# Decode attention with an MLP on one Trainium2 core: Wq loaded in column chunks, heads in h-major order, and the output projection's matmuls inside the loop

## The chip, the cores and the metric

The kernel runs on one core of one Trainium2 chip. The metric is the time of one execution on the device in microseconds (us), as the median of several runs; lower is better. "Span" is the length of the one execution that the profiler recorded.

## The reference

Four rows (a batch of 4, one new token each) go through a pre-norm attention block with a cache of 4096 keys and 32 heads of 128, then through an MLP with the Mish activation. All arrays are bf16. K and V are 134 MB each; they are nearly all of the 283.4 MB that the kernel has to read.

```python
def _A_ref(x, k_cache, v_cache, wq, wo):
    B, Sq, D = x.shape                      # 4, 1, 640
    H, Dh = 32, 128
    q = (x @ wq).reshape(B, Sq, H, Dh).transpose(0, 2, 1, 3)
    scores = jnp.einsum("bhqd,bhkd->bhqk", q, k_cache) * (Dh ** -0.5)
    p = _softmax(scores, axis=-1)
    o = jnp.einsum("bhqk,bhkd->bhqd", p, v_cache)
    return o.transpose(0, 2, 1, 3).reshape(B, Sq, H * Dh) @ wo

h  = x + _A_ref(_layernorm(x), k_cache, v_cache, wq, wo)
h2 = h + _B_ref(_layernorm(h), w1, b1, w2)  # 640 -> 1728, mish, -> 640
```

## The kernel before

There are 128 (row, head) pairs; I call each a head. For one head, K is a tile of 128 partitions with 32 keys each. VectorE multiplies it with the broadcast query and adds the 128 products of each key in a tree of halvings. ScalarE takes the exponential. TensorE multiplies with V and puts the four partial rows together. In cuts:

```python
wq_sb = big.tile([128, DC, H * Dh], BF16, tag="w40k")          # 40 KB a partition
nc.sync.dma_start(out=wq_sb, in_=A_wq...)                      # one DMA, ahead of K
...
for rnd in range(2):                                           # all of Q first
    for n in range(4):
        for c in range(DC): nc.tensor.matmul(qall_ps[...], xT[:, c, :], wq_sb[...])
    nc.vector.tensor_copy(out=Qall[...], in_=qall_ps)
wo_sb = big.tile([128, DC, H * Dh], BF16, tag="w40k")          # Wo takes Wq's place
...
heads = [(b, h) for b in range(N) for h in range(H)]
for idx, (b, h) in enumerate(heads):
    issue_qbc(idx + PRE)                                       # broadcast q to 128 partitions
    Kt = kt_pool.tile(...)   # 3 buffers, 1 MB, on the SyncE queue
    Vt = v_pool.tile(...)    # 3 buffers, 1 MB, on the ScalarE queue
    prod = work.tile([128, RC, Dh], BF16, tag="prod")          # 2 buffers
    nc.vector.tensor_tensor(out=prod, in0=Kt, in1=qbc..., op=ALU.mult)
    # tree: 128 -> 64 -> 32 -> 16 -> 8 -> 4 -> 2, then s_f32
    # ... exp, row sums, 8 PV matmuls, pvsb, 4 o matmuls, Orow
    if h == H - 1:           # once per row: reciprocal, 32 transposes -> OT_sb[:, :, b]
# behind the loop
for h in range(H):
    for (c0, c1) in ((0, 512), (512, D)):
        nc.tensor.matmul(yatt_ps[:, c0:c1], lhsT=OT_sb[:, h, :], rhs=wo_view[:, h, c0:c1], ...)
# ... h_rows, layernorm, MLP on 4 partitions x 1728, out
```

The program is written in this order, but the order in which each engine runs its instructions is made by a scheduler when the program is compiled.

The softmax here doesn't subtract the row's maximum and nothing guards it: scores larger than these inputs give would overflow.

Of the kernel before, what the change touches and what calls it, by code (L numbers as in the profile page):

```python
# [8 lines left out]
FP32 = mybir.dt.float32  # L9
BF16 = mybir.dt.bfloat16  # L10
# [5 lines left out]
def kernel(  # L16
# [13 lines left out]
    nc = tc.nc  # L30

    B, Sq, D = A_x.shape
    _, H, Sk, Dh = A_k_cache.shape
    F = B_w1.shape[1]
    N = B * Sq
    DC = D // 128
    RC = Sk // 128
    GP = 4
    NG = RC // GP
    SCALE = float(Dh) ** -0.5  # L40
    EPS = 1e-5

    consts = ctx.enter_context(tc.tile_pool(name="consts", bufs=1))
    big = ctx.enter_context(tc.tile_pool(name="big", bufs=1))
    work = ctx.enter_context(tc.tile_pool(name="work", bufs=2))
# [4 lines left out]
    x_bf = consts.tile([N, D], BF16)  # L50
    nc.sync.dma_start(out=x_bf[:, :], in_=x_rows[:, :])

    wq_sb = big.tile([128, DC, H * Dh], BF16, tag="w40k")
    nc.sync.dma_start(
        out=wq_sb[:, :, :], in_=A_wq.rearrange("(c p) n -> p c n", p=128)
    )

    ident = consts.tile([128, 128], BF16)
    make_identity(nc, ident[:, :])
    ident4 = ident[0:N, 0:N]  # L60

    ones_col = consts.tile([128, 1], FP32)
    nc.vector.memset(ones_col[:, :], 1.0)
# [5 lines left out]
    for b in range(N):  # L69
        nc.vector.tensor_copy(  # L70
            out=sel4[:, b, :], in_=ident[0:N, b : b + 1].to_broadcast([N, 128])
# [29 lines left out]
    def transpose_rows(rows_bf, colT_sb, nelems, ps_pool):  # L101
        nchunk = (nelems + 127) // 128
        tp_ps = ps_pool.tile([128, nchunk * N], FP32, tag="tp_ps")
        for c in range(nchunk):
            m = min(128, nelems - c * 128)
            nc.tensor.matmul(  # L106
                tp_ps[0:m, c * N : (c + 1) * N],
                lhsT=rows_bf[0:N, c * 128 : c * 128 + m],
                rhs=ident4,
                start=True,  # L110
                stop=True,
            )
        full_chunks = nelems // 128
        if full_chunks > 0:
            nc.vector.tensor_copy(
                out=colT_sb[:, 0:full_chunks, :],
                in_=tp_ps[:, 0 : full_chunks * N].rearrange("p (c n) -> p c n", n=N),
            )
        rem = nelems - full_chunks * 128
        if rem > 0:  # L120
            nc.vector.tensor_copy(
                out=colT_sb[0:rem, full_chunks, :],
                in_=tp_ps[0:rem, full_chunks * N : (full_chunks + 1) * N],
            )

    ln1_bf = consts.tile([N, D], BF16)
# [2 lines left out]
    xT = consts.tile([128, DC, N], BF16)  # L129
    Qall = consts.tile([N, H * Dh], BF16)  # L130

    with tc.tile_pool(name="ps_pro", bufs=1, space=bass.MemoryType.PSUM) as ps_pro:
        transpose_rows(ln1_bf, xT, D, ps_pro)
        QCOLS = 2048
        for rnd in range((H * Dh) // QCOLS):
            qall_ps = ps_pro.tile([N, QCOLS], FP32, tag="qall_ps")
            for n in range(QCOLS // 512):
                col0 = rnd * QCOLS + n * 512
                for c in range(DC):
                    nc.tensor.matmul(  # L140
                        qall_ps[:, n * 512 : (n + 1) * 512],
                        lhsT=xT[:, c, :],
                        rhs=wq_sb[:, c, col0 : col0 + 512],
                        start=(c == 0),
                        stop=(c == DC - 1),
                    )
            nc.vector.tensor_copy(  # L147
                out=Qall[:, rnd * QCOLS : (rnd + 1) * QCOLS], in_=qall_ps[:, :]
            )

    OT_sb = big.tile([128, H, N], BF16)

    wo_sb = big.tile([128, DC, H * Dh], BF16, tag="w40k")
    wo_view = wo_sb.rearrange("p c n -> p (c n)").rearrange("p (h n) -> p h n", h=H)
    w1_sb = big.tile([128, DC, F], BF16)
    w2_main_c = F // 128
# [1 line left out]
    w2_tail = big.tile([128, D], BF16)  # L158
    b1_bc = big.tile([N, F], BF16)

    did_late = {"done": False}

    def load_late_weights():
        if did_late["done"]:
            return
        did_late["done"] = True
        nc.sync.dma_start(
            out=wo_view[:, :, :], in_=A_wo.rearrange("(h p) n -> p h n", p=128)
        )
        nc.sync.dma_start(  # L170
            out=w1_sb[:, :, :], in_=B_w1.rearrange("(c p) n -> p c n", p=128)
        )
        nc.gpsimd.dma_start(
            out=w2_sb[:, :, :],
            in_=B_w2[0 : w2_main_c * 128, :].rearrange("(c p) n -> p c n", p=128),
        )
        rem_rows = F - w2_main_c * 128
        nc.gpsimd.dma_start(
            out=w2_tail[0:rem_rows, :], in_=B_w2[w2_main_c * 128 : F, :]
        )  # L180
        nc.gpsimd.dma_start(out=b1_bc[:, :], in_=B_b1.partition_broadcast(N))
# [5 lines left out]
    ps_cm = tc.tile_pool(name="ps_main", bufs=1, space=bass.MemoryType.PSUM)  # L187
    ps_main = ps_cm.__enter__()

    heads = [(b, h) for b in range(N) for h in range(H)]  # L190
    qbc_tiles = {}

    def issue_qbc(idx):
        if idx >= len(heads) or idx in qbc_tiles:
            return
        b, h = heads[idx]
        qbc_ps = ps_main.tile([128, 128], FP32, tag="qbc_ps")
        nc.tensor.matmul(  # L198
            qbc_ps[:, :],
            lhsT=sel4[:, b, :],  # L200
            rhs=Qall[:, h * Dh : (h + 1) * Dh],
            start=True,
            stop=True,
        )
        qbc_bf = work.tile([128, Dh], BF16, tag="qbc_bf", bufs=4)
        nc.scalar.copy(out=qbc_bf[:, :], in_=qbc_ps[:, :])  # L206
        qbc_tiles[idx] = qbc_bf

    PRE = 3
    for i in range(PRE):  # L210
        issue_qbc(i)

    lrow_ps = None
    Orow = None
    for idx, (b, h) in enumerate(heads):
        if h == 0:
            lrow_ps = ps_main.tile([1, H], FP32, tag="lrow_ps", bufs=2)
            Orow = work.tile([1, H, Dh], BF16, tag="Orow", bufs=2)

        issue_qbc(idx + PRE)  # L220

        Kt = kt_pool.tile([128, RC, Dh], BF16, tag="Kt")
        nc.sync.dma_start(
# [6 lines left out]
            in_=A_v_cache[b, h].rearrange("(p r) d -> p r d", p=128),  # L230
        )

        qbc = qbc_tiles[idx]
        prod = work.tile([128, RC, Dh], BF16, tag="prod")
        nc.vector.tensor_tensor(  # L235
            out=prod[:, :, :],
            in0=Kt[:, :, :],
            in1=qbc[:, :].unsqueeze(1).to_broadcast([128, RC, Dh]),
# [3 lines left out]
        width = Dh  # L242
        while width > 2:
            half = width // 2
            dst_dt = BF16
            nxt = work.tile([128, RC, half], dst_dt, tag=f"tree{half}")
            nc.vector.tensor_tensor(  # L247
                out=nxt[:, :, :],
                in0=cur[:, :, 0:half],
                in1=cur[:, :, half:width],  # L250
                op=ALU.add,
            )
            cur = nxt
            width = half
# [16 lines left out]
        )  # L271

        nc.tensor.matmul(  # L273
            lrow_ps[0:1, h : h + 1],
            lhsT=rowsum[:, :],
            rhs=ones_col[:, :],
            start=True,
# [2 lines left out]

        pv_ps = ps_main.tile([GP, GP * Dh], FP32, tag="pv_ps", bufs=2)
        for g in range(NG):
            nc.tensor.matmul(  # L283
                pv_ps[:, :],
                lhsT=e_bf[:, g * GP : (g + 1) * GP],
                rhs=Vt[:, g * GP : (g + 1) * GP, :],
                start=(g == 0),
                stop=(g == NG - 1),
            )
        pvsb = work.tile([GP, GP * Dh], BF16, tag="pvsb")  # L290
        nc.scalar.copy(out=pvsb[:, :], in_=pv_ps[:, :])  # L291

        o_ps = ps_main.tile([1, Dh], FP32, tag="o_ps", bufs=2)
        for i in range(GP):
            nc.tensor.matmul(  # L295
                o_ps[:, :],
# [2 lines left out]
                start=(i == 0),  # L299
                stop=(i == GP - 1),  # L300
            )
        nc.scalar.copy(out=Orow[0:1, h, :], in_=o_ps[0:1, :])  # L302

        if idx == 64:
            load_late_weights()

        if h == H - 1:
            rl = work.tile([1, H], FP32, tag="rl")
            nc.vector.reciprocal(out=rl[0:1, :], in_=lrow_ps[0:1, :])
            rl_bf = work.tile([1, H], BF16, tag="rl_bf")  # L310
            nc.vector.tensor_copy(out=rl_bf[0:1, :], in_=rl[0:1, :])
            ot_ps = ps_main.tile([128, H], FP32, tag="ot_ps")
            for hh in range(H):
                nc.tensor.matmul(
                    ot_ps[:, hh : hh + 1],
                    lhsT=Orow[0:1, hh, :],
                    rhs=rl_bf[0:1, hh : hh + 1],
                    start=True,
                    stop=True,
                )  # L320
            nc.vector.tensor_copy(out=OT_sb[:, :, b], in_=ot_ps[:, :])

    load_late_weights()
    ps_cm.__exit__(None, None, None)
    v_cm.__exit__(None, None, None)
    kt_cm.__exit__(None, None, None)
# [1 line left out]
    mlp = ctx.enter_context(tc.tile_pool(name="mlp", bufs=1))  # L328
    ps_epi = ctx.enter_context(tc.tile_pool(name="ps_epi", bufs=1, space=bass.MemoryType.PSUM))

    yatt_ps = ps_epi.tile([N, D], FP32, tag="acc1")
    for h in range(H):
        for (c0, c1) in ((0, 512), (512, D)):
            nc.tensor.matmul(  # L334
                yatt_ps[:, c0:c1],
                lhsT=OT_sb[:, h, :],
                rhs=wo_view[:, h, c0:c1],
                start=(h == 0),
                stop=(h == H - 1),
            )  # L340
    h_rows = mlp.tile([N, D], FP32)
    nc.vector.tensor_tensor(
        out=h_rows[:, :], in0=x_bf[:, :], in1=yatt_ps[:, :], op=ALU.add
# [45 lines left out]
    actT = mlp.tile([128, FC, N], BF16)  # L389
    transpose_rows(act_bf, actT, F, ps_epi)  # L390

    y2_ps = ps_epi.tile([N, D], FP32, tag="acc1")
    for (c0, c1) in ((0, 512), (512, D)):
        for c in range(FC):
            rows = min(128, F - c * 128)
# [46 lines left out]
```

## Time and profile before

| | before |
|---|---|
| median time | 746.65 us (4 runs) |
| span of the profiled run | 746.0 us |
| bytes moved | 283.8 MB |
| VectorE busy | 653.0 us (88%) |
| TensorE busy | 485.5 us (65%) |
| first product on VectorE | 45.9 us |
| last V has landed | 688.6 us |
| `h_rows` (attention done) starts | 706.35 us |

The page cuts the span into 40 equal slices of 18.65 us. The first two lines are busy tenths of VectorE (DVE) and of the DMA engines, the third is what the DMA moved in each slice.

```profile
DVE  1079999999989999999999999999989999998155
DMA  9989999999999999999999999999999999997000
GB/s 359 401 331 423 421 422 421 422 421 421 420 421 407 423 421 421 422 420 421 420 422 421 421 416 417 420 421 416 418 394 397 423 421 422 421 422 307 1 0 0
```

From the fourth slice to the 36th, the DMA is full and moves close to 421 GB/s (three slices have 394 to 407), and VectorE is nearly full too. So both are suspects for the bound of the loop, and the first and last slices are outside it.

The next view gives stretches of the span: start and end, length, then busy time of TensorE, its weight loads, VectorE, ScalarE and GpSimd with instruction counts, the granted clock, the DMA's busy share, and GB/s.

```profile
28.00:40.00 12.00, 7.85 (x27) 2.67 (x27) 2.28 (x1) 0.00 (x0) 0.00 (x0) 1.00 1.01 420
40.00:46.00 6.00, 3.28 (x16) 1.28 (x15) 2.38 (x2) 0.27 (x1) 0.00 (x0) 1.00 0.55 186
46.00:58.00 12.00, 1.41 (x7) 0.49 (x6) 12.00 (x17) 1.70 (x7) 0.00 (x0) 0.55 1.06 395
100.00:130.00 30.00, 21.08 (x94) 7.17 (x92) 30.00 (x49) 7.41 (x30) 0.00 (x0) 0.78 1.01 421
200.00:400.00 200.00, 142.91 (x660) 48.75 (x658) 193.92 (x326) 49.22 (x200) 0.00 (x0) 0.74 1.01 420
400.00:500.00 100.00, 70.94 (x303) 23.84 (x302) 96.04 (x161) 24.99 (x101) 0.00 (x0) 0.71 1.01 420
676.00:690.00 14.00, 10.23 (x46) 3.44 (x46) 10.70 (x22) 3.46 (x15) 0.00 (x0) 0.76 0.73 271
```

At 28 to 40 us VectorE uses no K at all and the DMA still moves 420. In the loop (200 to 400) it moves 420 as well. At 40 to 46 us it falls to 186. If 422 GB/s is what the DMA can do (the full slices show 420 to 423), the time that a stretch loses is its length times (1 - rate/422): 3.4 us here, 0.8 us in the next stretch, and 5.0 us at the very end.

Two lines of the timeline show the start (start, length, engine, line, operation, output <- inputs, and in brackets the idle time before it with what ended that):

```profile
29.78 6.36 PE L140 MATMUL qall_ps<-wq_sb,xT 128*4 128x512 bf16 x20 [25.15 <-DMA wq_sb<-in_A_wq_dram]
45.90 4.49 DVE L235 TENSOR_TENSOR prod<-Kt,qbc_bf 128x4096 bf16<-128x4096 bf16 x2 [0.60 <-ACT qbc_bf L206]
```

The first Q matmul waits for all of Wq, and the first product comes only at 45.9 us. And the end:

```profile
692.48 1.24 PE L283 MATMUL pv_ps<-Vt,e_bf 128*4 128x512 bf16 x5
695.73 10.53 PE L334 MATMUL yatt_ps<-wo_sb,OT_sb 128*4 128x512 bf16 x64 [0.32 <-DVE OT_sb L321]
706.35 0.81 DVE L342 TENSOR_TENSOR h_rows<-x_bf,yatt_ps 4x640 f32<-4x640 bf16 x1 [10.68 <-PE yatt_ps L334]
722.00 10.94 DVE L376 RECIPROCAL tb<-ta 4x1728 f32<-4x1728 f32 x1
```

The last PV matmuls end at 693.7, the 64 Wo matmuls stand in the open for 10.5 us, and the MLP follows. Nothing overlaps this tail.

A head's eight VectorE operations last 5.5 us added up (2.29 for the product, 1.22 to 0.19 for each of the others), and the schedule alternates the operations of two heads. The start times in the trace show neighbours of different heads overlapping by about 85 ns; where an operation follows its own producer (as a few do at the start and the end) there is a gap of 35 ns instead.

### The profile page before, as it was taken

Reading aid. Unit: us, or ns where it says so; the run is one execution under the profiler, and the core shown is the slowest. Engines: PE = TensorE matmul, PEld = TensorE weight load, DVE = VectorE, ACT = ScalarE, POOL = GpSimd, SP = SyncE. Lnnn points to the kernel's source line nnn. Section 1 sums busy time; section 2 is a strip of 40 time slices with the busy share of each in tenths; the row PEclk is TensorE's granted clock in tenths of the full one; section 3 lists DMA queues with packets and bytes.
Section 4 is the critical chain, followed back from the end, with each engine's and each line's share of the span. In section 5 each row is a group of like instructions: output and inputs, shape, how many; then the busy total and the mean of one; then the engine's idle time right before and its main releaser. Section 6 shows DMA issues by size and latency. Waiting matters only on the chain.

```text
span 746.0 us, 6937 instructions
## 1 busy us (share of the span) xinstructions
PE 485.5 (65%) x2224; PEld 167.9 (23%) x2224; DVE 653.0 (88%) x1066; ACT 166.4 (22%) x647; POOL 3.1 (0%) x9
## 2 busy tenths in 40 slices
PE   0335767667677676766676876767676676777823
PEld 0111222222222222222222222222222222222311
DVE  1079999999989999999999999999989999998155
ACT  0002222222222222222222222222222222222110
POOL 1000000000000000000000000000000000000000
PEclk9976687776667867777876568686888866677976
DMA  9989999999999999999999999999999999997000
GB/s 359 401 331 423 421 422 421 422 421 421 420 421 407 423 421 421 422 420 421 420 422 421 421 416 417 420 421 416 418 394 397 423 421 422 421 422 307 1 0 0
DMA packets 42836, 283.82 MB, mean 380 GB/s; under 512 B 4212, under 2 KB 8316, under 8 KB 9392
## 3 DMA queue, kind: packets, MB, share of 16 engines
q1 hardware_dynamic: 23872, 146.93, 47.9%
q10 hardware_dynamic: 18432, 134.23, 43.5%
q0 software_dynamic: 496, 2.23, 0.8%
q8 instruction: 17, 0.28, 0.1%
q14 instruction: 19, 0.16, 0.1%
HBM read 283.36 MB, written 0.01 MB: 380 GB/s over the span
## 4 chain that ended last, share of the span: by engine, by line
DMA 53%; PE 28%; DVE 10%; issue 5%; ACT 2%; ACTq 0%; SPq 0%; DVEq 0%
DMA Vt<-in_A_v_cache_dram 48%; PE pv_ps L283 20%; DVE nxt L247 5%; DMA wq_sb<-in_A_wq_dram 4%; PE o_ps L295 3%; DMA Kt<-in_A_k_cache_dram 2%; ACT pvsb L291 2%; DVE tb L376 1%; PE qall_ps L140 1%; PE yatt_ps L334 1%; PE y_ps L400 1%; DVE prod L235 1%; PE h_ps L355 1%; DVE Qall L147 1%; DVE s_f L256 0%
## 5 line engine op out<-in xcount | busy, mean ns | idle before, releaser
L283 PE MATMUL pv_ps<-Vt,e_bf 128*4 128x512 bf16 x1024 | 362.3, 508 | 104.7 <-DMA Vt<-in_A_v_cache_dram 104.6
L235 DVE TENSOR_TENSOR prod<-Kt,qbc_bf 128x4096 bf16<-128x4096 bf16 x128 | 293.3, 2292 | 12.4 <-DMA Kt<-in_A_k_cache_dram 11.1
L247 DVE TENSOR_TENSOR nxt<-nxt 128x1024 bf16<-128x1024 bf16 (+4 forms) x640 | 199.2, 364 | 0.2
L247 DVE TENSOR_TENSOR nxt<-prod 128x2048 bf16<-128x2048 bf16 x128 | 156.6, 1224 | 0.0
L283 PEld LDWEIGHTS <-e_bf 128*4 128x4 bf16 x1024 | 95.5, 99 | 266.3 <-issue 222.7
L291 ACT CAST pvsb<-pv_ps 4x512 bf16<-4x512 f32 x128 | 73.4, 573 | 242.5 <-PE pv_ps L283 241.4
L295 PE MATMUL o_ps<-pvsb,ident 4*1 4x128 bf16 x512 | 58.1, 243 | 44.9 <-ACT pvsb L291 44.9
L302 ACT CAST Orow<-o_ps 1x128 bf16<-1x128 f32 x128 | 32.5, 254 | 135.9 <-PE o_ps L295 134.3
L295 PEld LDWEIGHTS <-ident 4*1 4x1 bf16 x512 | 34.9, 85 | 90.9 <-issue 86.0
L265 ACT ACTIVATE e_bf<-s_f 128x32 bf16<-128x32 f32 x128 | 28.9, 226 | 93.6 <-DVE s_f L256 93.5
L273 PE MATMUL lrow_ps<-ones_col,rowsum 128*1 128x1 f32 x256 | 25.1, 167 | 33.0 <-ACT e_bf L265 33.0
L206 ACT CAST qbc_bf<-qbc_ps 128x128 bf16<-128x128 f32 x128 | 31.4, 245 | 59.2 <-PE qbc_ps L198 42.9
L198 PE MATMUL qbc_ps<-Qall,sel 4*128 4x128 bf16 x128 | 31.5, 246 | 17.4 <-ACT qbc_bf L206 15.0
L147 DVE CAST Qall<-qall_ps 4x2048 bf16<-4x2048 f32 x2 | 4.6, 2279 | 35.8 <-PE qall_ps L140 35.8
L273 PEld LDWEIGHTS lrow_ps<-ones_col,rowsum 128*1 128x1 f32 x256 | 15.2, 88 | 76.4 <-ACT e_bf L265 57.9
L140 PE MATMUL qall_ps<-wq_sb,xT 128*4 128x512 bf16 x40 | 10.8, 435 | 27.5 <-DMA wq_sb<-in_A_wq_dram 25.2
L198 PEld LDWEIGHTS <-sel 4*128 4x128 bf16 x128 | 11.9, 94 | 59.5 <-issue 55.4
L256 DVE TENSOR_TENSOR s_f<-nxt 128x32 f32<-128x32 bf16 x128 | 24.2, 189 | 0.2
L265 ACT ACTIVATION_READ_ACCUMULATOR e_bf<-s_f 128x1 f32 x128 | 23.8, 186 | 0.0
L106 PE MATMUL tp_ps<-ident,act_bf 4*128 4x4 bf16 (+1 forms) x14 | 0.6, 166 | 20.8 <-DVE act_bf L386 20.8
L140 PEld LDWEIGHTS <-xT 128*4 128x4 bf16 x40 | 3.8, 94 | 34.2 <-issue 30.1
L376 DVE RECIPROCAL tb<-ta 4x1728 f32<-4x1728 f32 x1 | 10.9, 10940 | 0.0
(49 smaller groups left out, 69.0 us busy)
## 6 DMA issues: line engine op xcount, KB each, us to landing
Vt<-in_A_v_cache_dram ACTq DMA_DIRECT2D x128, 1024.0 KB, 11.4
Kt<-in_A_k_cache_dram SPq DMA_DIRECT2D x128, 1024.0 KB, 12.4
wq_sb<-in_A_wq_dram SPq DMA_DIRECT2D x1, 5120.0 KB, 28.6
wo_sb<-in_A_wo_dram SPq DMA_DIRECT2D x1, 5120.0 KB
w_sb<-in_B_w_dram SPq DMA_DIRECT2D x1, 2160.0 KB, 36.6
w_sb<-in_B_w_dram POOLq DMA_DIRECT2D x1, 2080.0 KB, 24.5
w_tail<-in_B_w_dram POOLq DMA_DIRECT2D x1, 80.0 KB, 24.1
x_bf<-in_A_x_dram SPq DMA_DIRECT2D x1, 5.0 KB
```

Of the source, the lines that this page charges most:

```text
L140: nc.tensor.matmul(qall_ps[:, n * 512 : (n + 1) * 512], lhsT=xT[:, c, :], rhs=wq_sb[:, c, col0 : col0 + 512], start=(c == 0), stop=(c == D ...
L198: nc.tensor.matmul(qbc_ps[:, :], lhsT=sel4[:, b, :], rhs=Qall[:, h * Dh : (h + 1) * Dh], start=True, stop=True,)
L206: nc.scalar.copy(out=qbc_bf[:, :], in_=qbc_ps[:, :])
L235: nc.vector.tensor_tensor(out=prod[:, :, :], in0=Kt[:, :, :], in1=qbc[:, :].unsqueeze(1).to_broadcast([128, RC, Dh]), op=ALU.mult,)
L247: nc.vector.tensor_tensor(out=nxt[:, :, :], in0=cur[:, :, 0:half], in1=cur[:, :, half:width], op=ALU.add,)
L256: nc.vector.tensor_tensor(out=s_f32[:, :], in0=cur[:, :, 0], in1=cur[:, :, 1], op=ALU.add,)
L265: nc.scalar.activation(out=e_bf[:, :], in_=s_f32[:, :], func=ACT.Exp, scale=SCALE, accum_out=rowsum[:, :],)
L273: nc.tensor.matmul(lrow_ps[0:1, h : h + 1], lhsT=rowsum[:, :], rhs=ones_col[:, :], start=True, stop=True,)
L283: nc.tensor.matmul(pv_ps[:, :], lhsT=e_bf[:, g * GP : (g + 1) * GP], rhs=Vt[:, g * GP : (g + 1) * GP, :], start=(g == 0), stop=(g == NG - 1),)
L291: nc.scalar.copy(out=pvsb[:, :], in_=pv_ps[:, :])
L295: nc.tensor.matmul(o_ps[:, :], lhsT=ident[0:GP, i : i + 1], rhs=pvsb[:, i * Dh : (i + 1) * Dh], start=(i == 0), stop=(i == GP - 1),)
L302: nc.scalar.copy(out=Orow[0:1, h, :], in_=o_ps[0:1, :])
```

## The change

The intent: start the heads after one eighth of Wq, keep the DMA from running dry at the start, and take the Wo matmuls out of the tail. For that, heads go h-major, so that the four rows of one h are finished together. The core of the diff:

```diff
-    nc.sync.dma_start(out=wq_sb[:, :, :], in_=A_wq.rearrange("(c p) n -> p c n", p=128))
+    for n in range(NQC):                        # 8 chunks of 512 columns
+        nc.gpsimd.dma_start(out=wq_sb[:, :, n * 512 : (n + 1) * 512],
+            in_=A_wq[:, n * 512 : (n + 1) * 512].rearrange("(c p) n -> p c n", p=128))
...
-    wo_sb = big.tile([128, DC, H * Dh], BF16, tag="w40k")
+    wo_sb = big.tile([128, DC, H * Dh], BF16, tag="wo40k")     # a place of its own
+    # Wo, w1, w2, b1: all on the GpSimd queue
...
-    heads = [(b, h) for b in range(N) for h in range(H)]
+    heads = [(b, h) for h in range(H) for b in range(N)]
+    def ensure_qall(n): ...                     # Q for 512 columns, when a head needs it
...
-        prod = work.tile([128, RC, Dh], BF16, tag="prod")
+        prod = work.tile([128, RC, Dh], BF16, tag="prod", bufs=1)
-            nxt = work.tile([128, RC, half], dst_dt, tag=f"tree{half}")
+            nxt = work.tile([128, RC, half], BF16, tag=f"tree{half}", bufs=1)
...
+        if idx >= N - 1 + LAG and (idx - LAG) % N == N - 1:
+            finish_group((idx - LAG) // N, idx)    # reciprocal, 4 transposes -> OT_sb[:, h, :]
+        if idx >= 24 and yatt_next <= (idx - LAG - 2) // N - 1:
+            emit_yatt(yatt_next, idx)              # two Wo matmuls, tied behind a PV matmul
+            yatt_next += 1
...
-    for h in range(H):                             # 64 Wo matmuls behind the loop
-        for (c0, c1) in ((0, 512), (512, D)):
-            nc.tensor.matmul(yatt_ps[:, c0:c1], ...)
```

## The prediction

> **What bounds the kernel now.** The DMA. The page's 40 slices show 420 to 423 GB/s from 56 us to 670 us with DMA at 9 tenths, and 422 GB/s is also what the queues move in 28 to 40 us, when VectorE uses no K at all, so it is the DMA's own limit here [...]. 283.9 MB at 422 GB/s are 673 us. VectorE is close behind: one head's eight operations last 5.5 us added up, but the schedule alternates two heads, so that neighbours are independent and overlap by some 85 ns; a head then costs 4.85 us against 4.97 us of DMA for its 2.1 MB. Where an operation follows its own producer (a few places), a gap of 35 ns stands in place of the overlap.
>
> Outside the stream: start-up, where VectorE's first product waits until 45.9 us for all of Wq (landed at 29.8) and for the Q matmuls and casts; K and V buffers are full by then, and the DMA idles about 3.3 us (40 to 46 us by windows). At the end the last V lands at 688.6 us, PV for two backlogged heads runs to 693.8, the 64 Wo matmuls take 10.5 us (695.7 to 706.3), and the MLP another 39.7 us.
>
> **What the change does.** Same bytes. Wq comes in eight column chunks on the GpSimd queue, Q is made chunk by chunk, heads run h-major, Wo and MLP weights follow on the GpSimd queue, and Wo matmuls go into the loop.
>
> - Start: the GpSimd queue's first packets came at 6.6 us and it got 100 to 110 GB/s beside the two others. One chunk (0.66 MB) should land near 13 us (estimate), then 5 matmuls (2.1 us), copy 0.6, broadcast 0.5: first product near 17 us, not 45.9. Only the 3.3 us of DMA idleness count, since the DMA was otherwise busy.
> - Wo: 60 of 64 matmuls leave the tail: -9 us. PE has room (65% busy).
> - Slightly worse: 14.9 MB of short rows; with such rows in the mix the DMA moved 395 to 411 GB/s: +1 to 2 us.
> - VectorE: 32 short reciprocals, about 5 us in all, inside its slack. Earlier start gives it room: 1 to 2 us less hiccup (540 to 580 us ran at 397 GB/s) and less PE backlog at the end.
>
> [...]
>
> **Sum.** 746.65 - 9 - 3.3 - 3 + 1.5 = about 733 us, on the edge of 2%. Range 722 to 752. Faster by over 2%: 0.47; within 2%: 0.41; slower by over 2%: 0.12.
>
> **What would show it.** First product at 14 to 20 us; no idle DMA slice before the end; K/V progress slower than 5 us a head until the GpSimd queue is empty (about 100 us), then about 4.98; DMA ending near 684 us; h_rows some 8 us after the last V, not 17.7; the MLP tail unchanged near 40 us.
>
> **What would make it wrong.** The buffers of the product and the addition tree fall to one. If the order still alternates heads, nothing is lost: each tile is read before the next head writes it. If it becomes serial per head, a head costs about 5.7 us, VectorE bounds the loop, and the kernel reaches 780 to 800 us; in part serial, 5.1 to 5.3 us, it ends as before. Also a GpSimd queue that is served slower than I think, or reciprocals that make VectorE wait for PE.

## The result

The changed kernel takes 735.86 us (median of 10 runs, 733.82 to 736.8) against 747.15 us for the kernel before in the same rounds. The ratio is 0.9849 with a 95% interval of 0.9833 to 0.9866: faster by 1.5%, so within 2%. All ratios here are the mean time of one kernel's fast runs over that of the other's fast runs of the same rounds, so they are not quite the ratio of the medians quoted. The numerical result is correct.

The slices of the changed kernel (18.3 us each):

```profile
DVE  1996766999999999999999999999999999999564
DMA  8999999999999999999999999999999999999300
GB/s 342 418 423 422 423 414 392 421 421 421 421 421 420 422 419 422 420 422 419 416 421 422 421 413 421 419 393 422 419 419 418 414 421 417 410 415 403 121 0 0
```

Its stretches, at the same times as before:

```profile
28.00:40.00 12.00, 6.63 (x26) 1.87 (x26) 12.00 (x21) 3.76 (x10) 0.54 (x1) 1.00 1.02 418
40.00:46.00 6.00, 2.51 (x16) 0.94 (x16) 6.00 (x11) 1.50 (x8) 0.00 (x0) 1.00 1.02 427
46.00:58.00 12.00, 7.99 (x31) 2.66 (x31) 11.59 (x22) 1.73 (x10) 0.00 (x0) 0.72 1.02 425
100.00:130.00 30.00, 17.56 (x73) 5.73 (x70) 20.74 (x34) 6.00 (x27) 0.00 (x0) 0.65 1.02 399
200.00:400.00 200.00, 145.83 (x666) 52.23 (x666) 194.02 (x328) 49.70 (x211) 0.00 (x0) 0.76 1.01 420
400.00:500.00 100.00, 73.84 (x329) 26.10 (x329) 96.51 (x163) 24.56 (x105) 0.00 (x0) 0.74 1.00 414
676.00:690.00 14.00, 11.90 (x66) 4.65 (x65) 8.88 (x22) 4.34 (x17) 0.00 (x0) 0.77 0.54 191
```

The hole at 40 to 46 us is gone: 427 GB/s instead of 186. The loop moves the same 420. But 100 to 130 us now has 399 (before: 421), and 400 to 500 has 414 (before: 420); by the formula these cost 1.6 and 1.4 us more than before. (The kernel before has a weak stretch of its own at another place, the slices with 394 and 397 at 541 to 578 us.) The start and the end in the timeline:

```profile
15.90 2.29 PE L200 MATMUL qall_ps<-wq_sb,xT 128*4 128x512 bf16 x5 [10.11 <-DMA wq_sb<-in_A_wq_dram]
19.45 2.29 DVE L300 TENSOR_TENSOR prod<-Kt,qbc_bf 128x4096 bf16<-128x4096 bf16 x1 [13.09 <-ACT qbc_bf L223]
```

```profile
689.24 1.24 PE L347 MATMUL pv_ps<-Vt,e_bf 128*4 128x512 bf16 x5
692.35 0.43 PE L261 MATMUL yatt_ps<-wo_sb,OT_sb 128*4 128x512 bf16 x2 [0.25 <-ACT OT_sb L257]
692.82 0.81 DVE L388 TENSOR_TENSOR h_rows<-x_bf,yatt_ps 4x640 f32<-4x640 bf16 x1 [4.35 <-PE yatt_ps L261]
```

Three times put the gain in its place:

| | before | changed | difference |
|---|---|---|---|
| last V landed (last packet of its queue) | 688.6 | 687.6 | -1.0 |
| from there to the start of `h_rows` | 17.7 | 5.2 | -12.5 |
| from the start of `h_rows` to the end | 39.7 | 40.1 | +0.4 |
| span | 746.0 | 732.9 | -13.1 |

So the first product came 26 us earlier, but the stream of K and V ended only 1 us earlier. Added up from the two traces, what the DMA has moved by a given time puts the changed kernel ahead by 4.2 us (at 422 GB/s) at 100 us, 2.6 at 130, 2.8 at 476, 1.6 at 495, 3.8 at 580 and still 2.7 at 676. Another 1.7 us go at the very end, where the DMA is no longer full (busy 0.54 at 676 to 690 us; before 0.73): the last V is issued only when the PV matmuls of an earlier head have freed its buffer, at 683.14 us (those matmuls end at 683.04); before at 684.17 (684.00).

Nearly all of the gain is in the open tail: the Wo block (10.5 us before; two matmuls, 0.43 us together, stand there now), and TensorE is closer behind V (last PV 5.1 us after the last V before, 2.9 us now).

VectorE waits for K in both kernels, and more so now, mostly while the weights share the DMA (at 100 to 130 us it is busy 20.74 of 30 us, before 30.00). The columns are waiter, what it waited for, us in total, times, longest; first the kernel before, then the changed one:

```profile
DVE prod L235 <- DMA Kt<-in_A_k_cache_dram: 11.1, 36, 0.7
```

```profile
DVE prod L300 <- DMA Kt<-in_A_k_cache_dram: 33.5, 40, 2.8
```

### The profile page after: what moved, and what is told of

The parts are those of the page before. It is cut to its first block, busy times and chain, and to the rows that moved or that the text cites. A ratio compares the mean times of both kernels' runs of the same rounds, so it can differ in the third digit from the quotient of the medians.

```text
span 732.9 us, 7047 instructions
## 1 busy us (share of the span) xinstructions
PE 487.5 (67%) x2224; PEld 173.2 (24%) x2224; DVE 653.1 (89%) x1084; ACT 169.8 (23%) x687; POOL 12.7 (2%) x19
## 4 chain that ended last, share of the span: by engine, by line
DMA 66%; PE 23%; DVE 6%; ACT 3%; issue 2%; ACTq 0%; POOL 0%; POOLq 0%
DMA Vt<-in_A_v_cache_dram 64%; PE pv_ps L347 19%; DMA wq_sb<-in_A_wq_dram 2%; ACT pvsb L355 2%; PE o_ps L359 2%; DVE tb L422 1%; DVE nxt L311 1%; DVE prod L300 1%; PE y_ps L446 1%; PE h_ps L401 1%; PE qall_ps L200 0%; DVE act_bf L432 0%; DVE tb L413 0%; DVE h L409 0%; ACT e_bf L329 0%
## 5 line engine op out<-in xcount | busy, mean ns | idle before, releaser
L347 PE MATMUL pv_ps<-Vt,e_bf 128*4 128x512 bf16 x1024 | 356.3, 506 | 127.6 <-DMA Vt<-in_A_v_cache_dram 127.6
L311 DVE TENSOR_TENSOR nxt<-nxt 128x1024 bf16<-128x1024 bf16 (+4 forms) x640 | 201.5, 361 | 0.3 <-issue 0.2
L347 PEld LDWEIGHTS <-e_bf 128*4 128x4 bf16 x1024 | 98.5, 100 | 295.4 <-issue 248.4
L359 PE MATMUL o_ps<-pvsb,ident 4*1 4x128 bf16 x512 | 57.0, 240 | 40.6 <-ACT pvsb L355 40.5
L337 PE MATMUL grp_ps<-ones_col,rowsum 128*1 128x1 f32 x256 | 24.3, 164 | 16.3 <-ACT e_bf L329 15.9
L223 ACT CAST qbc_bf<-qbc_ps 128x128 bf16<-128x128 f32 x128 | 31.5, 246 | 13.0 <-DVE prod L300 10.9
L337 PEld LDWEIGHTS grp_ps<-ones_col,rowsum 128*1 128x1 f32 x256 | 12.4, 82 | 44.9 <-ACT e_bf L329 28.9
L200 PE MATMUL qall_ps<-wq_sb,xT 128*4 128x512 bf16 x40 | 12.7, 458 | 10.1 <-DMA wq_sb<-in_A_wq_dram 10.1
L261 PE MATMUL yatt_ps<-wo_sb,OT_sb 128*4 128x512 bf16 x64 | 17.5, 366 | 0.2 <-ACT OT_sb L257 0.2
L250 PE MATMUL grp_ps<-rl,Orow 1*128 1x1 bf16 x128 | 9.6, 165 | 3.6 <-DVE rl L246 1.8
L422 DVE RECIPROCAL tb<-ta 4x1728 f32<-4x1728 f32 x1 | 10.9, 10941 | 0.0
## 6 DMA issues: line engine op xcount, KB each, us to landing
Kt<-in_A_k_cache_dram SPq DMA_DIRECT2D x128, 1024.0 KB, 12.5
```

Of the source, the lines that this page charges most:

```text
L223: nc.scalar.copy(out=qbc_bf[:, :], in_=qbc_ps[:, :])
L311: nc.vector.tensor_tensor(out=nxt[:, :, :], in0=cur[:, :, 0:half], in1=cur[:, :, half:width], op=ALU.add,)
L337: nc.tensor.matmul(grp_ps[0:1, N + b : N + b + 1], lhsT=rowsum[:, :], rhs=ones_col[:, :], start=True, stop=True,)
L347: anchors_pe[idx] = nc.tensor.matmul(pv_ps[:, :], lhsT=e_bf[:, g * GP : (g + 1) * GP], rhs=Vt[:, g * GP : (g + 1) * GP, :], start=(g == 0) ...
L359: nc.tensor.matmul(o_ps[:, :], lhsT=ident[0:GP, i : i + 1], rhs=pvsb[:, i * Dh : (i + 1) * Dh], start=(i == 0), stop=(i == GP - 1),)
L422: nc.vector.reciprocal(out=tb[:, :], in_=ta[:, :])
```

## The experiments

Twelve kernels ran. The differences between them and the changed kernel are taken from their ratios to the kernel before (0.01 is about 7.5 us), since they ran in different rounds. By the intervals of the two ratios, such a difference is uncertain by 2 to 3 us.

### 1. Wo matmuls back in the tail (first try)

```diff
-        if idx >= 24 and yatt_next <= (idx - LAG - 2) // N - 1:
+        if False and yatt_next <= (idx - LAG - 2) // N - 1:
```

> The changed kernel with all 64 Wo matmuls put back behind the loop, everything else as changed. Theory (most of the gain is the Wo block leaving the exposed tail): the time rises by 8.5 to 10 us over the changed kernel, to 744 to 747 us, ratio to before 0.996 to 1.000; h_rows starts some 15 us after the last V instead of 5.2. Rival (the gain comes from the earlier start of the heads): it rises by 3 us at most, to 736 to 739 us.

Measured: 736.16 us, ratio 0.9851, the same as the changed kernel. By its number the rival would have won. The scheduler had drawn the Wo matmuls back between the heads (from 85 us on, in the changed kernel from 177), because their inputs are ready and nothing ties them to the end. The run did not test what it meant to. It shows one thing: the ties in the change ("hold Wo matmuls back") are not what makes the Wo matmuls overlap.

### 2. Wo matmuls really in the tail

```diff
-        if idx >= 24 and yatt_next <= (idx - LAG - 2) // N - 1:
+        if False and yatt_next <= (idx - LAG - 2) // N - 1:
...
-        emit_yatt(yatt_next, None)
+        emit_yatt(yatt_next, NH - 1)               # tied behind the last PV matmul
```

> The changed kernel with all 64 Wo matmuls tied behind the last PV matmul. The run a_tail had only moved them in the program text, and the scheduler had drawn them into the loop again; here the compiled order has been looked at and they do stand after the last PV. Theory (taking the Wo block out of the exposed tail is the main gain): 8.5 to 10 us over the changed kernel, 744 to 746 us, ratio 0.996 to 0.999. Rival (the gain lies elsewhere): at most 3 us over it.

Measured: 742.36 us, ratio 0.9948, 7.4 us over the changed kernel by ratio. The timeline:

```profile
692.67 7.55 PE L261 MATMUL yatt_ps<-wo_sb,OT_sb 128*4 128x128 bf16 x55
700.26 0.81 DVE L388 TENSOR_TENSOR h_rows<-x_bf,yatt_ps 4x640 f32<-4x640 bf16 x1 [11.59 <-PE yatt_ps L261]
```

`h_rows` starts at 700.26 instead of 692.82, 7.4 us later, and the last V is where it was (687.6). The Wo block is thus the largest piece of the change's gain, but it is worth 7.4 us here and not 9: 9 of the 64 matmuls already fit in gaps before the last transposes, and the 55 left take 7.55 us (0.137 us each), while the kernel before needed 10.5 us for 64 (0.165 us each, at a granted clock of 0.84).

### 3. All of Q first

```diff
     PRE = 3
+    for n in range(NQC):
+        ensure_qall(n)
     for i in range(PRE):
         issue_qbc(i)
```

> The changed kernel with all eight Q chunks computed before the first head, so that the first product waits for all of Wq (about 40 us instead of 19.5). Theory (only idle DMA time counts, and the GpSimd queue still has Wo and the MLP weights to move while K and V are full): 0 to +2 us over the changed kernel, 735 to 738 us, ratio 0.985 to 0.988; the DMA shows no idle slice. Rival (VectorE's start time counts): +15 to +20 us, 751 us or more.

Measured: 735.42 us, ratio 0.9836 (changed kernel: 0.9849, the intervals overlap). The first product is 20 us later than in the changed kernel, and it costs nothing:

```profile
40.09 2.29 DVE L302 TENSOR_TENSOR prod<-Kt,qbc_bf 128x4096 bf16<-128x4096 bf16 x1 [34.62 <-ACT qbc_bf L223]
```

```profile
28.00:40.00 12.00, 8.44 (x26) 2.42 (x25) 0.00 (x0) 3.09 (x6) 0.00 (x0) 1.00 1.02 411
40.00:46.00 6.00, 1.47 (x6) 0.58 (x6) 5.85 (x4) 1.38 (x6) 0.00 (x0) 0.59 1.02 420
46.00:58.00 12.00, 4.86 (x17) 1.36 (x17) 12.00 (x21) 3.20 (x9) 0.00 (x0) 0.50 1.02 412
```

The DMA moves 411 to 420 GB/s all the while, since the GpSimd queue still has Wo and the MLP weights to bring (until 72 us). So, with the weights on a queue of their own, starting the heads early is not what pays, and computing Q in chunks could be left out. The DMA was kept full by loads that wait for no head.

### 4 and 5. The kernel before with single buffers, and with a place of its own for Wo

The single buffers were needed to make room for Wo, so they ran alone as a control.

```diff
# b_bufs1
-        prod = work.tile([128, RC, Dh], BF16, tag="prod")
+        prod = work.tile([128, RC, Dh], BF16, tag="prod", bufs=1)
-            nxt = work.tile([128, RC, half], dst_dt, tag=f"tree{half}")
+            nxt = work.tile([128, RC, half], dst_dt, tag=f"tree{half}", bufs=1)
-            Orow = work.tile([1, H, Dh], BF16, tag="Orow", bufs=2)
+            Orow = work.tile([1, H, Dh], BF16, tag="Orow", bufs=1)
# b_woslot: as b_bufs1, and
-    wo_sb = big.tile([128, DC, H * Dh], BF16, tag="w40k")
+    wo_sb = big.tile([128, DC, H * Dh], BF16, tag="wo40k")
```

> The kernel before with one buffer each for the product, the tree tiles and Orow, nothing else. Control for the next run, and a test of the risk that the prediction named. Theory (the schedule still alternates two heads): within 0.4% of before. Rival (one buffer makes the heads serial): a head costs about 5.7 us, 800 us or more.

Measured: 740.78 us, ratio 0.9914 (0.9895 to 0.9933). The control was meant to change nothing and gained 6.5 us. VectorE's order still alternates two heads, so the risk that the prediction named did not come about. But the loop moved 426 GB/s where the kernel before moved 420. That rate had been taken for the DMA's own limit. Experiments 10 and 11 follow from this.

> The kernel before with one buffer each as in the control, and with a slot of its own for Wo, so that Wo needs not wait for Wq's last reader and fills the idle DMA of 40 to 46 us. Theory (the stream is DMA-bound, every idle microsecond of the start counts): 2 to 4 us less than the control, ratio to before 0.995 to 0.998, the last V 3 us earlier. Rival (the changed kernel has no idle start either and yet its last V came only 1 us earlier, so VectorE's and PE's pace sets the end): within 1 us of the control, the idle time reappears later in the stream.

Measured: 743.3 us, ratio 0.9937 (0.9914 to 0.9959), 1.7 us slower than the control by ratio. The six runs spread from 740.26 to 746.02 us and the two intervals overlap, so "slower" is not shown and the rival (within 1 us) is not excluded; but a gain of 2 to 4 us would have been seen, and here the theory fell. The edit also did more than was meant: the scheduler issued Wo at 5.8 us, and the 2160 KB of w1, which the control has issued at about 6 us, only at 61.7. In the profiled run, which at 746.02 us is the slowest of the six, the hole was filled and came back later:

```profile
40.00:46.00 6.00, 2.92 (x14) 1.13 (x13) 3.02 (x2) 0.53 (x2) 0.00 (x0) 1.00 1.06 396
46.00:58.00 12.00, 1.36 (x6) 0.39 (x4) 11.93 (x15) 2.17 (x6) 0.00 (x0) 0.50 0.78 282
58.00:100.00 42.00, 27.28 (x114) 8.49 (x114) 35.19 (x62) 9.34 (x37) 0.00 (x0) 0.70 0.95 379
```

At 40 to 46 us the DMA now moves 396 GB/s, but 282 at 46 to 58 and 379 at 58 to 100: by the formula 0.4, 4.0 and 4.3 us. The control lost 4.1, 0.8 and nothing at these places (133, 393 and 422 GB/s). When the first product starts (45.3 us), K's and V's three buffers are full, and the first V buffer is not free until its PV has run. In the control, as in the kernel before, Wo was loaded in just that time. My reading, argued from these two traces: the hole is a debt of the pipeline's filling, and whatever independent load is spent before it is missing in it. The changed kernel has 14.9 MB of weights on a third queue that last until 127 us, and has no hole at either place.

### 6. Less work for VectorE (a failed experiment)

```diff
-        width = Dh
+        width = Dh // 2        # the second half of the product is never added
```

> The changed kernel without the first tree level (the second half of the product is not added; the result is wrong on purpose): VectorE loses 1.14 us of 4.85 us a head. Theory (the stream is bound by the DMA): 1 to 4 us less than the changed kernel, 732 to 735 us, since only the last head's latency and some jitter go. Rival (VectorE is the bound, or both bind about equally): 30 us less or more.

Measured: 801.38 us, ratio 1.0743: less work, and some 66 us slower than the changed kernel. (The result even passes the comparison with the reference, so passing it shows little here.) The run does not answer its question, for the compiler's scheduler knew the shorter operations and made another order on all engines. VectorE's own waits:

```profile
DVE prod L300 <- ACT qbc_bf L223: 158.7, 75, 12.9
```

VectorE waits 158.7 us for broadcast queries (changed kernel: 13.8 us, of which 13.1 is the start). One such wait in the timeline:

```profile
311.72 0.58 ACT L355 CAST pvsb<-pv_ps 4x512 bf16<-4x512 f32 x1 [8.82 <-PE pv_ps L347]
312.20 0.25 ACT L223 CAST qbc_bf<-qbc_ps 128x128 bf16<-128x128 f32 x1
312.48 2.29 DVE L300 TENSOR_TENSOR prod<-Kt,qbc_bf 128x4096 bf16<-128x4096 bf16 x1 [4.24 <-ACT qbc_bf L223]
```

ScalarE's cast of the query now stands behind a cast of a PV result that has waited 8.82 us for a late V, and the product waits for both. And between 200 and 600 us, 283 of 521 VectorE operations follow the one before with a gap of 20 to 120 ns, as if behind their own producer (35 ns in the kernel before); in the changed kernel 21 of 654 do, 20 of them behind a short reciprocal. So this is what the serial order that the prediction feared looks like. It costs 5.6 us a head, waits included.

### 7. Less V

```diff
-            out=Vt[:, :, :],
-            in_=A_v_cache[b, h].rearrange("(p r) d -> p r d", p=128),
+            out=Vt[:, 0:24, :],
+            in_=A_v_cache[b, h].rearrange("(p r) d -> p r d", p=128)[:, 0:24, :],
...
-        for g in range(NG):
+        for g in range(6):
```

> The changed kernel loading and using only three quarters of V (wrong result on purpose): 33.6 MB less, 80 us at 422 GB/s. Theory (VectorE is close behind the DMA: 19.5 us start plus 128 heads of 4.85 us ends at 640 us): 38 to 46 us less than the changed kernel, 690 to 698 us, with VectorE busy 97% and the DMA no longer full. Rival (the DMA alone bounds): 75 to 80 us less. Second rival (VectorE bounds): less than 5 us.

Measured: 705.69 us, ratio 0.946, some 29 us less than the changed kernel. The middle of the loop:

```profile
200.00:400.00 200.00, 126.76 (x614) 44.40 (x613) 199.77 (x343) 53.28 (x218) 0.00 (x0) 0.72 0.97 375
```

VectorE is busy 199.8 of 200 us and the DMA falls to 375 GB/s: now VectorE is the bound, at 4.87 us a head by the starts of its products (changed kernel: 5.04). So both rivals fall and the theory stands, with a size too large: VectorE starts at 17.8, but waits for K while the weights are loaded (its last product comes at 651.7), which the sum of start and 128 heads had left out. Of the 5.04 us a head of the changed kernel, 0.17 us is all that VectorE leaves.

### 8. Wq on the SyncE queue

```diff
-        nc.gpsimd.dma_start(out=wq_sb[:, :, n * 512 : (n + 1) * 512], ...)
+        nc.sync.dma_start(out=wq_sb[:, :, n * 512 : (n + 1) * 512], ...)
```

> The changed kernel with the eight Wq chunks issued on the SyncE queue ahead of K, not on the GpSimd queue. Theory (the queue that carries the weights does not matter as long as the DMA is full): within 2 us of the changed kernel, ratio 0.982 to 0.988, although the first product comes at another time. Rival (the GpSimd queue is what makes the start cheap, because K is not behind Wq): 4 us or more slower.

Measured: 742.67 us, ratio 0.9957, about 8 us slower than the changed kernel by ratio. The theory (the queue does not matter) fell, and the rival held. SyncE's timeline:

```profile
1.15 41.44 SPq L63 DMA_DIRECT2D wq_sb<-in_A_wq_dram  x8
42.64 16.35 SPq L288 DMA_DIRECT2D Kt<-in_A_k_cache_dram  x5
```

Issuing the eight chunks took SyncE 41.4 us; the first K could not be issued before 42.6, and the first product came at 52.2. Rows of 1 KB are not in themselves slow to issue: the first two chunks took 0.41 and 0.51 us, the next four 4.8 to 12.5 us each, the last two 2.3 and 2.5 us. What held them no run shows. On the GpSimd queue the same eight took GpSimd 1.05 + 6.12 us:

```profile
1.28 1.05 POOL L63 DMA_DIRECT2D wq_sb<-in_A_wq_dram  x1 [0.34 <-issue]
2.66 6.12 POOL L63 DMA_DIRECT2D wq_sb<-in_A_wq_dram  x7
24.17 1.16 POOL L172 DMA_DIRECT2D w_sb<-in_B_w_dram  x1 [1.32 <-DMA wq_sb<-in_A_wq_dram]
```

And the other weights on the GpSimd queue were through at 40.6 us, so that nothing independent was left when the pipeline filled. By the formula the next stretch alone lost 7.4 us:

```profile
58.00:100.00 42.00, 23.86 (x116) 8.30 (x116) 41.98 (x73) 10.96 (x40) 0.00 (x0) 0.87 0.88 348
```

The last line of GpSimd's timeline also shows that a busy VectorE did not hold up this issue: the 2080 KB load at 24.17 us took 1.16 us to issue while VectorE ran a product (23.65 to 25.93 us); the same load at 1.29 us in the kernel before, with VectorE nearly idle, took 1.33 us. The gaps between GpSimd's later issues (7.3, 4.2, 1.3, 0.5 and 3.7 us) each end with a DMA of Wq, not with VectorE.

### 9. The MLP on 128 partitions

The cost of the open tail was to be shown by cutting it where it is longest. The hidden layer is made transposed, so that the 1728 values of a row lie on 128 partitions, not on one. (The removed lines are summed up in two comments.)

```diff
-    # h1[4, 1728] += h2T[:, c, :]^T w1[:, c, cols]      (20 matmuls)
-    # six elementwise steps on [4, 1728], then 14 transposes
+    for fc in range(FC):                       # 14 chunks; the last takes the last 128 columns
+        f0 = min(fc * 128, F - 128)
+        for c in range(DC):
+            nc.tensor.matmul(h1_ps[:, fc, :], lhsT=w1_sb[:, c, f0 : f0 + 128],
+                             rhs=h2T[:, c, :], start=(c == 0), stop=False)
+        nc.tensor.matmul(h1_ps[:, fc, :], lhsT=b1_bc[0:1, f0 : f0 + 128],
+                         rhs=sel4[0:1, 0, 0:N], start=False, stop=True)   # + b1 (a row of ones)
+    # the same steps on [128, 14, 4]; the last writes actT itself
```

> The changed kernel with the MLP's hidden layer made with features on the 128 partitions (14 chunks of 128 x 4) instead of 4 partitions x 1728, so that the six elementwise steps (20.5 us in the trace, 10.9 of it one reciprocal) become some 0.2 us each and the 14 transposes go; 84 small matmuls replace 20. Theory (the tail is exposed in full, so each microsecond taken from it counts): 15 to 18 us less than the changed kernel, 718 to 721 us, ratio 0.961 to 0.965. Rival (part of it comes back as matmul time with 128-column weights): 8 to 12 us less.

Measured: 716.19 us, ratio 0.9601 (0.957 to 0.9633), correct; 18.5 us less than the changed kernel by ratio. The reciprocal that took 10.94 us is now:

```profile
703.38 0.50 DVE L429 RECIPROCAL tb<-ta 128x56 f32<-128x56 f32 x1
```

What was taken from the tail came off the time, as the theory had it (it expected 15 to 18 us).

### 10 and 11. Where the K and V buffers start

In the compiled program the first K buffer of the kernel before starts at byte 161,664 of each partition, 384 past a multiple of 512; in the changed kernel at 172,992 (448 past one). In the control of experiment 4, which moved 426 GB/s, it is at 137,216, an exact multiple. All K and V buffers are 8 KB long, so they share this offset.

```diff
-    eps_t = consts.tile([N, 1], FP32)
+    eps_wide = consts.tile([N, 40], FP32)      # before: 128 B more (changed kernel: [N, 24], 64 B)
+    eps_t = eps_wide[:, 0:1]
```

> The kernel before with one constant tile made 128 B longer, so that the K and V buffers start at a multiple of 512 B in each partition (before: 384 B past one). No instruction changes. Theory (the control b_bufs1 streamed at 426 instead of 421 GB/s because its buffers happened to fall on multiples of 512 B): the loop runs at 425 to 427 GB/s, 5 to 8 us less than before, ratio 0.990 to 0.993. Rival (the single buffers of the tree, another order on VectorE, made the control faster): within 1 us of before.

> The changed kernel with one constant tile made 64 B longer, so that the K and V buffers start at a multiple of 512 B (changed kernel: 448 B past one). No instruction changes. Theory (alignment of the destination): 425 to 427 GB/s in the loop instead of 419 to 421, 5 to 8 us less than the changed kernel, 728 to 731 us, ratio 0.975 to 0.978. Rival (the h-major order of addresses in memory holds the changed kernel at 421 GB/s): within 1 us of the changed kernel.

Measured: the kernel before went to 738.49 us, ratio 0.9894 (0.9865 to 0.9922); the changed kernel to 729.19 us, ratio 0.977 (0.9742 to 0.9799), 5.9 us less than without the padding. The order of instructions is the same on all engines. The middle of the loop, first the padded kernel before, then the padded changed kernel:

```profile
200.00:400.00 200.00, 147.38 (x669) 48.70 (x670) 196.93 (x331) 50.00 (x203) 0.00 (x0) 0.71 1.01 426
```

```profile
200.00:400.00 200.00, 144.69 (x666) 52.00 (x666) 197.03 (x333) 49.86 (x211) 0.00 (x0) 0.77 1.01 426
```

Both move 426 GB/s instead of 420. So both rivals fall: neither the single buffers nor the h-major order of addresses plays a part in the rate. The padding moves all tiles behind the constant, so strictly the runs show "these tiles' addresses"; K and V are nearly all of the traffic.

The padding that helps K and V hurts the start of the changed kernel, first unpadded, then padded:

```profile
6.00:28.00 22.00, 4.38 (x13) 1.38 (x14) 8.84 (x11) 2.43 (x8) 7.08 (x8) 1.00 1.00 403
```

```profile
6.00:28.00 22.00, 4.37 (x13) 1.39 (x14) 8.86 (x11) 2.44 (x8) 7.06 (x8) 1.00 1.01 389
28.00:40.00 12.00, 7.28 (x25) 1.98 (x25) 12.00 (x21) 3.19 (x9) 0.54 (x1) 1.00 1.01 394
```

At 6 to 28 us the rate falls from 403 to 389, and at 28 to 40 from 418 to 394: the same 64 B moved the Wq tile from 28,928 (256 past a multiple of 512) to 28,992 (320 past one), and Wq's rows are short (1 KB). Wo does the same: its tile went from 69,888 (256 past) to 69,952 (320 past), and at 46 to 82 us, where Wo comes in beside K and V, the DMA moved 423 GB/s in the changed kernel and 413 in the padded one, although K and V themselves were better placed there. That the weights' addresses are the reason was not tested alone.

Why the offset matters no run here shows. The rate of the loop rose by 1.4% (420 to 426 GB/s) in both kernels, from an offset of 384 B in the one and 448 B in the other; no offset of K and V between 0 and 384 B was tried.

### 12. Both improvements (the edits of 9 and 11 together)

> The changed kernel with both: aligned K and V buffers and the MLP on 128 partitions. Theory (one shortens the stream, the other the exposed tail, so they add up): 709 to 712 us, ratio 0.950 to 0.955. Rival (with a faster stream VectorE becomes the bound and gives part back): 713 to 716 us.

Measured: 710.38 us (709.91 to 712.7), ratio 0.9526 (0.9495 to 0.9557), correct. The two add up: 5.6 us less than experiment 9 by ratio. This version beats the kernel before by 4.7% and the changed kernel by about 3.3%.

| kernel | median us | ratio to before |
|---|---|---|
| changed kernel | 735.86 | 0.9849 |
| 1 Wo later in the text only | 736.16 | 0.9851 |
| 2 Wo in the tail | 742.36 | 0.9948 |
| 3 all of Q first | 735.42 | 0.9836 |
| 4 before, single buffers | 740.78 | 0.9914 |
| 5 before, single buffers, place for Wo | 743.3 | 0.9937 |
| 6 less VectorE work, another order | 801.38 | 1.0743 |
| 7 three quarters of V | 705.69 | 0.946 |
| 8 Wq on SyncE's queue | 742.67 | 0.9957 |
| 9 MLP on 128 partitions | 716.19 | 0.9601 |
| 10 before, aligned | 738.49 | 0.9894 |
| 11 changed, aligned | 729.19 | 0.977 |
| 12 changed, aligned, MLP on 128 partitions | 710.38 | 0.9526 |

## Why the prediction was right or wrong

The predicted time was 733 us and the measured one 735.86, inside the range; "faster by over 2%" had the largest chance by a little, and the outcome was "within 2%". The mechanism held, but two terms and one premise of the sum were off. That the sum came so close is in part luck, for the two errors nearly cancel: the last V landed at 687.6 us, 3.6 later than the "near 684 us" of the prediction, and `h_rows` came 5.2 us after it, 2.8 sooner than the "some 8 us".

- **"first product near 17 us, not 45.9"; "Only the 3.3 us of DMA idleness count".** It came at 19.45 us, and the first half of the sentence's logic is shown by experiment 3: with the first product at 40.1 us the time is the same. The size failed: the stream's end moved by 1.0 us, where the hole alone should have given 3.3. The changed kernel was ahead by 4.2 us when the hole was filled; 1.6 went at 100 to 130 us, where the last of the weights come in (the GpSimd queue ends at 126.6 us, not at "about 100"), and 1.7 in the last 12 us, where V's buffers and not the DMA set the pace. The "1 to 2 us less hiccup" did not come off: the weak stretch of the kernel before at 541 to 578 us is gone, but others stand in its place, the largest at 476 to 495, so that the lead at 676 us is what it was at 130. The cause of these stretches stays open; so does how much of the smaller backlog at the end belongs to which part of the change.
- **"60 of 64 matmuls leave the tail: -9 us."** Right in kind: the block in the tail went from 10.5 us to 0.43, and putting it back cost 7.4 us (experiment 2). In addition the backlog of TensorE behind the last V shrank more than allowed for: `h_rows` comes 5.2 us after the last V, where the prediction said "some 8 us".
- **"VectorE: 32 short reciprocals, about 5 us in all, inside its slack", "PE has room".** Held. VectorE is busy 653.1 us (before 653.0), the 32 reciprocals take 5.2 us (164 ns each) and wait 3.2 us in all, once, at the very end.
- **"+1 to 2 us" for short rows.** The size was met, 1.6 us more lost than before at 100 to 130 us, but not for the reason given. Wo and w2 have rows of the same 1280 B on the same queue; with Wo beside K and V the DMA moved 423 GB/s (46 to 82 us), with w2 403 (106 to 118 us). So rows of 1280 B alone are not slow here. The tile of Wo starts 256 B past a multiple of 512, that of w2 (128,128) 128 B past one; that the address is the cause is my estimate from these two rates and those of experiment 11, and no run moved w2 alone. (In the kernel before, Wo came on SyncE's queue and in single rows, packets of 1280 B, at 395 GB/s (46 to 58 us); the GpSimd queue moved it four rows to a packet, 5120 B.)
- **"it is the DMA's own limit here".** This premise was wrong by 1.4%, in both kernels alike, which is why it did no harm to the difference. With the K and V buffers off a multiple of 512 B the loop moved 420 GB/s; with everything shifted so that they start at one it moves 426 (experiments 4, 10, 11). That the DMA moved the same 420 at 28 to 40 us, when VectorE used no K, made it look confirmed; but the K buffers filled then had the same offset, so it could not tell a free DMA from a hindered one.
- **"If the order still alternates heads, nothing is lost."** Held: with single buffers the order still alternates, in the changed kernel and in experiment 4. Experiment 6 showed by accident what happens when it does not: 5.6 us a head.
- **"K/V progress ... then about 4.98."** 5.04 us a head by the starts of the products, as in the kernel before (5.04 to 5.05): a miss, small for one head, but some 6 us over a hundred. The aligned kernels of experiments 10 and 11 come to 4.97.

## What to carry to other kernels

Where the DMA bounded the loop, as here, an earlier start of compute was worth at most the time in which the DMA had nothing to do, and here even less (1.0 of 3.3 us, for a first product 26 us earlier), because the lead was spent again before the end. In these runs that time was covered by loads that depend on nothing and come through a queue of their own, spread over the whole filling of the pipeline (427 GB/s at 40 to 46 us instead of 186); where such loads ended early (experiments 5 and 8), a hole opened a few microseconds later (282 GB/s at 46 to 58 us, 348 at 58 to 100). What stood in the open behind the stream counted in full (experiment 2: `h_rows` 7.4 us later, the time 7.4 us longer by ratio), so look there first: a reciprocal on 4 partitions cost as much (10.9 us) as all the Wo matmuls (10.5 us). And check where compiled programs put the buffers and the instructions: a control that "changes nothing" moved the buffers and gained more than half of what the change did, a term of the prediction was right in size for another reason, and an experiment that moved instructions behind the loop in the text left them in the loop in the compiled order.
